# Experts sorted by token count with windows of 232 to 168 columns, and up projections as pairs of a double-width and a single-width matmul

## The chip, the cores and the metric

One core of one Trainium2 chip. The metric is device microseconds (us) of one execution, the median of several; lower is better. The core's engines run their own instruction queues in order and wait for one another through semaphores: PE (TensorE, matmuls, with its weight loads PEld), DVE (VectorE), ACT (ScalarE), POOL (GpSimd), and SP, which issues most of the transfers.

## The reference, cut to what matters

Three stages follow one another; each takes the output of the one before. The middle one is the subject.

```python
attn_out = _attn_ref(q, k, v, lam)                  # decay attention, 2 x 8 heads x 768 x 64
x = attn_out.transpose(0, 2, 1, 3).reshape(1536, 512)
# _moe_ref: N, D, E, F = 1536, 512, 8, 1024
expert_idx = np.argmax(x @ w_gate, axis=1)          # each token goes to one of 8 experts
for e in range(E):
    mask = expert_idx == e
    h = np.maximum(x[mask] @ w1[e], 0.0)            # "up", 512 -> 1024
    out[mask] = gate_w[mask, None] * (h @ w2[e])    # "down", 1024 -> 512
# _moe2_ref: h = x @ w_in (512 -> 2048), Mish, @ w_out
```

## The kernel before

Attention runs until about 87 us. As it goes, tokens are routed: each row of its output is scattered by an indirect transfer into a DRAM table `bins` with one region per expert, in order of arrival. The MoE stage runs from 86.9 to 262.9 us, the FFN from there to 531.5 us.

An fp32 product is made of three products in a faster format: each operand is split into a high part (`hi`, ACT, L189) and the rest (`lo`, DVE or POOL, L194), and hi*hi, hi*lo and lo*hi are summed in PSUM. Weights come in pieces of 128x1024 (`raw`, `load_piece`, L182), eight for an expert, alternately of w1 and w2.

Each expert works on a fixed window of 232 token columns (`WIN`). The loop over g = 4*e + c (e the expert, c a quarter of its 1024 hidden columns) records for each g, in this order:

- `up(g)`: 24 matmuls of 232 columns (L719) into one PSUM tile `h` of tag "a", of which there are three. Then ACT writes relu of it as the high part of `hh` (L722) and DVE the low part (L723).
- at c = 3 the second half of the next expert's transposes (`turn_x(e+1, 1)`).
- `down(g-1)`: eight pairs of matmuls. The first (L740) takes the high weights against `hh` high and low side by side, 464 columns, into the two halves of a PSUM tile `y`; the second (L743) takes the low weights against `hh` high, 232 columns, into the second half. At c = 3 ACT copies one half to the sums `Y` (L747) and DVE adds the other (L748), four times.
- at g = 1 `clear_y` (L619 to L623: two memsets of `Y` on DVE, one each on ACT and POOL), the `pad` scatters that write zeros behind each expert's tokens (POOL), at c = 2 the first half of the next expert's transposes: `turn_x` (PE transposes L701 into a PSUM tile of tag "c", of which there is one; ACT L266 and DVE L267 split it), `advance` (the splits of two weight pieces), `load_x` (L689, the next expert's 256 rows of `bins` into `xw`), and for 9 values of g from 8 to 24 with c = 0 or 1 a conversion of FFN weights (`narrow`: ACT L139, DVE L140, L141, L146).

`tables()` (L647 to L664), 13 small DVE instructions, stands ahead of the loop, and computes offsets and slots from the counts. The buffers of weights and other large tiles are 33 units in rotation, so a load waits for the last reader of the unit that it takes. All engines take their instructions in the order in which they are recorded. An expert with more tokens than its window is finished by a loop behind the program's end; with this input's counts (195, 205, 194, 205, 168, 157, 227, 185) it isn't entered.

Of the kernel before, what the change touches and what calls it, by code (L numbers as in the profile page):

```python
# [39 lines left out]
REST = WIN - P  # L40
FF = 2048
# [5 lines left out]
NX = -(-NT // WIN) - 1  # L47
# [13 lines left out]
def kernel(  # L61
# [52 lines left out]
    cmax = const.tile([P, NE], F32, name="cmax")  # L114
# [50 lines left out]
    with tc.manual_schedule():  # L165
# [9 lines left out]

        def load_piece():
# [93 lines left out]
        with ExitStack() as actx:  # L270
# [95 lines left out]
            def constants():  # L366
                for i, (n, b) in enumerate(STEPS):
                    POOL.iota(tok[:, i:i + 1], pattern=[[0, 1]], base=b * SEQ + n * P, channel_multiplier=1)
                POOL.iota(
                    steps, pattern=[[WIN, NX]], base=WIN, channel_multiplier=0, allow_small_or_imprecise_dtypes=True)  # L370
# [3 lines left out]
                POOL.memset(ones8, 1.0)  # L374
                POOL.memset(zeros, 0.0)
# [210 lines left out]
            for _ in range(5):  # L586
                load_piece()
# [58 lines left out]

        def tables():  # L647
            DVE.tensor_tensor_scan(out=incl, data0=ones8, data1=base, initial=0.0, op0=ALU.mult, op1=ALU.add)
            DVE.tensor_tensor(out=off_f, in0=incl, in1=base, op=ALU.subtract)
# [357 lines left out]
```

## Time and profile before

| | |
|---|---|
| time, 3 runs | 542.29 us median (541.59 to 542.36) |
| profiled execution | 541.75 us, of which the span of the trace is 540.1 us |
| PE busy | 522.6 us (97%) |
| DVE, ACT, POOL busy | 369.8 (68%), 324.7 (60%), 185.2 us (34%) |
| DMA | 74.98 MB, mean 139 GB/s |

PE's share is that of the whole span. What DVE and ACT do matters where PE waits for them; the rows below show where that is, and how long single instructions take.

### The profile page before, as it was taken

How to read it: one execution, taken by the hardware profiler on the slowest of the kernel's cores; microseconds unless marked ns; L12 is line 12 of the kernel's file. 1: busy time of each engine (PE TensorE's matmuls, PEld its weight loads, DVE VectorE, ACT ScalarE, POOL GpSimd, SP SyncE). 2: the span in 40 equal slices, each digit the busy share in tenths (PEclk: the TensorE clock that was granted, in tenths of full speed). 3: DMA queues.
4: the chain of work that ended last, by engine and by line, in shares of the span. 5: the costliest groups of instructions: out<-in, count | busy, mean ns of one | idle time of the engine just before them, and what ended most of it. 6: DMA issues, size and time to landing. Idle time of an engine off the chain costs nothing. (4 is left out here: it accounts for less than half of the span.)

```text
span 540.1 us, 8441 instructions
## 1 busy us (share of the span) xinstructions
PE 522.6 (97%) x3101; PEld 451.4 (84%) x3102; DVE 369.8 (68%) x668; ACT 324.7 (60%) x514; POOL 185.2 (34%) x151
## 2 busy tenths in 40 slices
PE   8999988999999999999999999999999999999993
PEld 5888878999999999999788878888888888888882
DVE  7999965765967858653498776567965778436362
ACT  1566533655674566555678876777666775765650
POOL 7788842755573331235100321003210031103032
PEclk9999999999999999999999999999999999999997
DMA  8999837119999996731301024020230000001022
GB/s 259 340 329 332 277 147 292 52 49 399 315 299 224 223 360 236 262 128 40 118 0 62 18 79 133 23 79 0 95 139 4 0 0 1 0 1 58 21 80 81
DMA packets 28944, 74.98 MB, mean 139 GB/s; under 512 B 6652, under 2 KB 6652, under 8 KB 28896
## 3 DMA queue, kind: packets, MB, share of 16 engines
q1 hardware_dynamic: 25040, 66.62, 38.3%
q0 software_dynamic: 3424, 7.23, 3.6%
q8 instruction: 26, 0.43, 0.4%
q10 hardware_dynamic: 432, 0.53, 0.3%
q14 instruction: 22, 0.18, 0.1%
HBM read 66.61 MB, written 10.49 MB: 143 GB/s over the span
## 5 line engine op out<-in xcount | busy, mean ns | idle before, releaser
L194 POOL TENSOR_TENSOR lo_f<-w,hi_f 128x1024 fp32r<-128x1024 f32 x16 | 39.8, 2487 | 185.9 <-ACT hi_f L189 155.1
L719 PE MATMUL h<-x,hi_w 128*128 128x232 f32 x512 | 87.5, 274 | 0.0
L740 PE MATMUL y<-hh,hi_w 128*128 128x464 f32 x256 | 84.8, 380 | 0.9 <-DVE hh L723 0.9
L796 PE MATMUL hp<-yt,hi_f 128*128 128x512 f32 x256 | 79.3, 391 | 0.0
L719 PEld LDWEIGHTS h<-x,hi_w 128*128 128x128 f32 x512 | 77.8, 192 | 0.0
L828 PE MATMUL acc<-hi_f,ghi 128*128 128x512 f32 x192 | 76.2, 397 | 0.4 <-ACT Y L833 0.4
L828 PE MATMUL acc<-hi_f,glo 128*128 128x512 f32 x192 | 75.8, 395 | 0.0
L828 PE MATMUL acc<-lo_f,ghi 128*128 128x512 f32 x192 | 75.7, 394 | 0.0
L136 DVE TENSOR_TENSOR t<-t,hp 128x512 f32<-128x512 f32 x48 | 32.8, 684 | 61.1 <-ACT t L135 61.1
L719 PE MATMUL h<-x,lo_w 128*128 128x232 f32 x256 | 71.1, 278 | 0.0
L743 PE MATMUL y<-hh,lo_w 128*128 128x232 f32 x256 | 69.1, 270 | 0.0
L194 DVE TENSOR_TENSOR lo_w<-raw,hi_w 128x1024 fp32r<-128x1024 f32 x50 | 63.0, 1283 | 7.5 <-ACT hi_w L189 6.9
L132 ACT ACTIVATE t<-hp 128x512 f32<-128x512 f32 x48 | 28.6, 600 | 62.4 <-PE hp L796 62.1
L189 ACT ACTIVATE hi_w<-raw 128x1024 fp32r<-128x1024 f32 x64 | 64.5, 1055 | 0.9 <-DMA raw<-in_w1p_dram 0.9
L194 POOL TENSOR_TENSOR lo_w<-raw,hi_w 128x1024 fp32r<-128x1024 f32 x14 | 35.1, 2510 | 71.5 <-ACT hi_w L189 70.8
L796 PEld LDWEIGHTS hp<-yt,hi_f 128*128 128x128 f32 x256 | 48.1, 188 | 11.1
L740 PEld LDWEIGHTS y<-hh,hi_w 128*128 128x128 f32 x256 | 48.2, 188 | 6.1 <-DVE hh L723 1.1
L796 PE MATMUL hp<-yt,lo_f 128*128 128x512 f32 x128 | 50.4, 394 | 0.0
L719 PEld LDWEIGHTS h<-x,lo_w 128*128 128x128 f32 x256 | 49.0, 191 | 0.5
L743 PEld LDWEIGHTS y<-hh,lo_w 128*128 128x128 f32 x256 | 48.9, 191 | 0.0
L722 ACT ACTIVATE hh<-h 128x464 fp32r<-128x464 f32 x32 | 17.8, 558 | 49.7 <-PE h L719 45.2
L723 DVE SCALAR_TENSOR_TENSOR hh<-h,hh 128x464 fp32r<-128x464 f32 x32 | 20.4, 639 | 34.8 <-ACT hh L722 34.8
(163 smaller groups left out, 1032.9 us busy)
## 6 DMA issues: line engine op xcount, KB each, us to landing
raw<-in_w1p_dram SPq DMA_DIRECT2D x32, 512.0 KB
raw<-in_w2p_dram SPq DMA_DIRECT2D x32, 512.0 KB
w<-in_w3p_dram SPq DMA_DIRECT2D x32, 512.0 KB
xw<-bins SPq DMA_DIRECT2D x7, 512.0 KB
qbd<-in_qT_dram SPq DMA_DIRECT2D x24, 128.0 KB
v_n<-in_vN_dram SPq DMA_DIRECT2D x12, 256.0 KB
k_n<-in_kN_dram SPq DMA_DIRECT2D x10, 256.0 KB
k_t<-in_kT_dram SPq DMA_DIRECT2D x10, 256.0 KB
```

Source lines behind the costliest of these rows:

```text
L132: yield lambda: ACT.activation(out=t, in_=h, func=AF.Tanh, scale=0.5)
L136: yield lambda: DVE.tensor_tensor(out=t, in0=t, in1=h, op=ALU.mult)
L189: ACT.activation(out=hi, in_=r, func=AF.Copy)
L194: engine.tensor_tensor(out=lo, in0=r, in1=hi.bitcast(F32), op=ALU.subtract)
L719: PE.matmul(out=p[:, m, :], lhsT=w[:, s], rhs=x[k // 2][:, k % 2, r, :], start=(k == 0 and m == 0 and z == 0), stop=(k == KD - 1 and z == ...
L722: ACT.activation(out=h[:, :, 0, :], in_=p, func=AF.Relu)
L723: DVE.scalar_tensor_tensor(out=h[:, :, 1, :], in0=p, scalar=0.0, in1=h[:, :, 0, :].bitcast(F32), op0=ALU.max, op1=ALU.subtract)
L740: PE.matmul(out=y.rearrange("p z n -> p (z n)"), lhsT=whi[:, s], rhs=h[:, f].rearrange("p z n -> p (z n)"), start=(c == 0 and f == 0), sto ...
L743: PE.matmul(out=y[:, 1, :], lhsT=wlo[:, s], rhs=h[:, f, 0, :], start=False, stop=(c == 3 and f == 1), skip_group_check=True)
L796: PE.matmul(out=p, lhsT=w[:, s], rhs=x, start=(k == 0 and z == 0), stop=(k == KD - 1 and z == 2))
L828: PE.matmul(out=acc[t], lhsT=x[:, s], rhs=w[:, DM:2 * DM], start=(first and z == 0), stop=(last and z == 2))
```

## The change

The windows become `WINS = (232, 232, 232, 212, 200, 192, 180, 168)`. Experts 0 and 1 stay; the other six are taken by falling count, so that place 2 is the expert with most tokens. Which expert stands at a place is known on the chip alone, so `tables()` computes it (23 DVE instructions; those for left-over tokens are moved to g = 26), and SP loads `who_i` into registers and addresses weights and `bins` with them.

`up` now makes eight pairs like those of `down`: the first 128 hidden columns (m = 0) into one PSUM tile of tag "a", the second (m = 1) into another. Of each tile ACT copies one half to SBUF (L794) and DVE adds the other (L795); then come ACT's relu (L796) and DVE's low part (L797), now from that SBUF tile. `down` follows two groups behind instead of one. The transposes of expert 1 are both recorded at g = 2; those of later experts one group earlier than before (c = 1 and 2). Two weight pieces instead of five are preloaded at the end of attention.

```diff
-                for k0 in range(0, KD, 2):
-                    for m in range(2):
-                        for k in (k0, k0 + 1):
-                            s = slice(k * FC + m * P, k * FC + (m + 1) * P)
-                            for z, (w, r) in enumerate(((wlo, 0), (whi, 0), (whi, 1))):
-                                PE.matmul(out=p[:, m, :], lhsT=w[:, s], rhs=x[k // 2][:, k % 2, r, :],
...
-                ACT.activation(out=h[:, :, 0, :], in_=p, func=AF.Relu)
+                w = WINS[e]
+                h = hs[g] = ep.tile([P, 2, 2, WIN], F32R, tag="h", name=f"hh{g}", bufs=3)[:, :, :, 0:w]
+                p = [ps.tile([P, 2, WIN], F32, tag="a", name=f"h{g}_{m}", bufs=3)[:, :, 0:w] for m in range(2)]
+                t = ep.tile([P, 2, WIN], F32, tag="t", name=f"hs{g}", bufs=2)[:, :, 0:w]
+                for m in range(2):
+                    for k in range(KD):
+                        s = slice(k * FC + m * P, k * FC + (m + 1) * P)
+                        xk = x[k // 2][:, k % 2]
+                        PE.matmul(out=p[m], lhsT=whi[:, s], rhs=xk, start=(k == 0), stop=False,
+                                  skip_group_check=True)
+                        PE.matmul(out=p[m][:, 1, :], lhsT=wlo[:, s], rhs=xk[:, 0, :],
+                                  start=False, stop=(k == KD - 1), skip_group_check=True)
+                    ACT.activation(out=t[:, m, :], in_=p[m][:, 1, :], func=AF.Copy)
+                    DVE.tensor_tensor(out=t[:, m, :], in0=p[m][:, 0, :], in1=t[:, m, :], op=ALU.add)
+                ACT.activation(out=h[:, :, 0, :], in_=t, func=AF.Relu)
...
-            for g in range(NG + 1):
+            for g in range(NG + 2):
                 if g < NG:
                     up(g)
-                    if g % 4 == 3:
-                        turn_x(g // 4 + 1, 1)
-                if g > 0:
-                    down(g - 1)
+                if g > 1:
+                    down(g - 2)
...
+                    if g == 2:
+                        turn_x(1, 0)
+                        turn_x(1, 1)
+                    elif g > 4 and g % 4 in (1, 2):
+                        turn_x(g // 4 + 1, g % 4 - 1)
                     advance(2 * g + 7)
-                    if g % 4 == 0 and g > 0:
-                        load_x(g // 4 + 1)
+                    if g == 4:
+                        load_x(2)
+                    elif g > 4 and g % 4 == 3:
+                        load_x(g // 4 + 2)
```

On PE, around the transposes of expert 1 (`t_0`, `t_1`; `xw` are its rows), before: between the two stand the 24 matmuls of up(3), of which the first is shown.

```order
L701 MATMUL t_0_1432<-ident,xw_1248 128x128
L701 MATMUL t_0_1432<-ident,xw_1248 128x104
L701 MATMUL t_0_1432<-ident,xw_1248 128x128
L701 MATMUL t_0_1432<-ident,xw_1248 128x104
L719 MATMUL h_1448<-x_0_1221,lo_w_868 128x232
...
L701 MATMUL t_1_1476<-ident,xw_1248 128x128
```

The same place after, behind down(0):

```order
L771 MATMUL t_0_1434<-ident,xw_1262 128x128
L771 MATMUL t_0_1434<-ident,xw_1262 128x104
L771 MATMUL t_0_1434<-ident,xw_1262 128x128
L771 MATMUL t_0_1434<-ident,xw_1262 128x104
L771 MATMUL t_1_1442<-ident,xw_1262 128x128
L771 MATMUL t_1_1442<-ident,xw_1262 128x104
L771 MATMUL t_1_1442<-ident,xw_1262 128x128
L771 MATMUL t_1_1442<-ident,xw_1262 128x104
L790 MATMUL h_0_1458<-x_0_1235,hi_w_887 128x464
```

The second transposes follow the first at once now, and both use the one PSUM tile of tag "c".

On DVE, the first rows behind `tables()`, before (`h_...` the PSUM tiles of up(0), up(1) and up(2), `x_0` the split of `t_0`):

```order
L723 SCALAR_TENSOR_TENSOR hh_1269<-h_1270,hh_1269 128x2x232
L723 SCALAR_TENSOR_TENSOR hh_1309<-h_1310,hh_1309 128x2x232
L621 MEMSET Y_1237 128x1768
L622 MEMSET Y_1238 128x1768
L194 TENSOR_TENSOR lo_w_1374<-raw_865,hi_w_1373 128x1024
L194 TENSOR_TENSOR lo_w_1378<-raw_952,hi_w_1377 128x1024
L723 SCALAR_TENSOR_TENSOR hh_1381<-h_1382,hh_1381 128x2x232
L267 TENSOR_TENSOR x_0_1431<-t_0_1432,x_0_1431 128x2x232
```

The same place after (`hs` is the SBUF tile of the sums):

```order
L795 TENSOR_TENSOR hs_1334<-h_0_1332,hs_1334 128x232
L795 TENSOR_TENSOR hs_1334<-h_1_1333,hs_1334 128x232
L797 SCALAR_TENSOR_TENSOR hh_1331<-hs_1334,hh_1331 128x2x232
L650 MEMSET Y_1251 128x1768
L651 MEMSET Y_1252 128x1768
L221 TENSOR_TENSOR lo_w_1374<-raw_885,hi_w_1373 128x1024
L221 TENSOR_TENSOR lo_w_1378<-raw_972,hi_w_1377 128x1024
L795 TENSOR_TENSOR hs_1384<-h_0_1382,hs_1384 128x232
L795 TENSOR_TENSOR hs_1384<-h_1_1383,hs_1384 128x232
L797 SCALAR_TENSOR_TENSOR hh_1381<-hs_1384,hh_1381 128x2x232
L294 TENSOR_TENSOR x_0_1433<-t_0_1434,x_0_1433 128x2x232
L294 TENSOR_TENSOR x_1_1441<-t_1_1442,x_1_1441 128x2x232
```

The order is the old one with two adds ahead of each low part; `x_1` now stands directly behind `x_0`.

On DVE after, in a group of expert 3 with c = 1 (up(13), then the sums of expert 2, four adds of L822 of which one is shown, then the transposes of expert 4):

```order
L795 TENSOR_TENSOR hs_2155<-h_0_2153,hs_2155 128x212
L795 TENSOR_TENSOR hs_2155<-h_1_2154,hs_2155 128x212
L797 SCALAR_TENSOR_TENSOR hh_2152<-hs_2155,hh_2152 128x2x212
...
L822 TENSOR_TENSOR Y_1251<-y_0_1980,Y_1251 128x232
...
L294 TENSOR_TENSOR x_0_2220<-t_0_2221,x_0_2220 128x2x200
L221 TENSOR_TENSOR lo_w_2231<-raw_2129,hi_w_2230 128x1024
L221 TENSOR_TENSOR lo_w_2237<-raw_2135,hi_w_2236 128x1024
L155 TENSOR_SCALAR sb_2147<-w_1_1_1854 128x512
L156 SCALAR_TENSOR_TENSOR sb_2147<-w_1_1_1854,sb_2147 128x512
L161 SCALAR_TENSOR_TENSOR w_1_2146<-w_1_2146,sb_2147 128x512
```

Before, the split `x_0` stood a group later, with fewer instructions beside it, and there were no adds of L795.

## Rows read from the trace of the kernel before

**Rows 1.** PE, PEld, DVE, ACT, POOL busy in 20 us of MoE; PEclk, DMA share, GB/s:

```profile
140.00:160.00 20.00, 20.00 (x159) 19.41 (x158) 14.98 (x20) 11.29 (x19) 14.75 (x9) 1.00 0.97 310
```

**Rows 2.** Timeline of PE, within up: start, us, instructions:

```profile
113.21 0.27 PE L719 MATMUL h<-x,lo_w 128*128 128x232 f32 x1
...
113.55 0.27 PE L719 MATMUL h<-x,lo_w 128*128 128x232 f32 x1
```

**Rows 3.** Timeline of PE, within down:

```profile
110.31 0.38 PE L740 MATMUL y<-hh,hi_w 128*128 128x464 f32 x1
110.52 0.27 PE L743 MATMUL y<-hh,lo_w 128*128 128x232 f32 x1
110.62 0.38 PE L740 MATMUL y<-hh,hi_w 128*128 128x464 f32 x1
```

**Rows 4.** Timeline of PE's weight loads, same place:

```profile
110.31 0.19 PEld L743 LDWEIGHTS y<-hh,lo_w 128*128 128x128 f32 x1
...
110.63 0.19 PEld L743 LDWEIGHTS y<-hh,lo_w 128*128 128x128 f32 x1
```

**Rows 5.** Timeline of PE, first matmuls and the same line later:

```profile
2.47 3.60 PE L288 MATMUL idle<-warm 128*128 128x512 bf16 x8 [2.47 <-DVE warm L285]
5.86 4.83 PE L393 MATMUL a<-qbd,k_t 128*128 128x256 f32 x16
24.41 1.97 PE L393 MATMUL a<-qbd,k_t 128*128 128x256 f32 x8
```

**Rows 6.** Timeline of PE, first matmul of the MoE and first of down:

```profile
86.93 0.43 PE L719 MATMUL h<-x,lo_w 128*128 128x232 f32 x1
...
93.57 0.48 PE L740 MATMUL y<-hh,hi_w 128*128 128x464 f32 x1 [0.91 <-DVE hh L723]
```

**Rows 7.** Timeline of DVE, start of the MoE; in brackets idle time before, and releaser:

```profile
88.47 0.17 DVE L648 TENSOR_TENSOR_SCAN incl<-ones,base 128x8 f32<-128x8 f32 x1
...
90.66 0.17 DVE L664 TENSOR_TENSOR pos_i<-pos_f,slot_f 128x12 int32<-128x12 f32 x1
92.87 1.19 DVE L723 SCALAR_TENSOR_TENSOR hh<-h,hh 128x464 fp32r<-128x464 f32 x2 [2.04 <-ACT hh L722]
94.38 1.53 DVE L621 MEMSET Y<- 128x1768 f32 x1 [0.32 <-issue]
...
97.68 2.29 DVE L194 TENSOR_TENSOR lo_w<-raw,hi_w 128x1024 fp32r<-128x1024 f32 x2
```

**Rows 8.** Timeline of ACT, first relu of the MoE:

```profile
92.28 1.00 ACT L722 ACTIVATE hh<-h 128x464 fp32r<-128x464 f32 x2 [4.41 <-DMA raw<-in_w1p_dram]
```

**Rows 9.** Timeline of SP: the rows of experts 1 and 2, merged:

```profile
92.56 27.29 SPq L689 DMA_DIRECT2D xw<-bins  x2
```

**Rows 10.** Engines' busy time behind the last matmul, columns as in rows 1:

```profile
533.50:534.00 0.50, 0.00 (x0) 0.00 (x0) 0.00 (x0) 0.00 (x0) 0.00 (x0) 0.92 0.11 41
534.00:534.50 0.50, 0.00 (x0) 0.00 (x0) 0.00 (x0) 0.00 (x0) 0.00 (x0) 0.50 0.96 360
```

**Rows 11.** Last matmul, from the timeline of PE:

```profile
531.11 0.40 PE L828 MATMUL acc<-lo_f,ghi 128*128 128x512 f32 x1
```

**Rows 12.** Groups by line of DVE and ACT, 100 to 260 us: busy, mean ns:

```profile
L194 DVE TENSOR_TENSOR lo_w<-raw,hi_w 128x1024 fp32r<-128x1024 f32 x40 | 51.0, 1302 | 7.5 <-ACT hi_w L189 6.9 <-issue 0.6
...
L189 ACT ACTIVATE hi_w<-raw 128x1024 fp32r<-128x1024 f32 x54 | 54.1, 1055 | 0.0
L722 ACT ACTIVATE hh<-h 128x464 fp32r<-128x464 f32 x29 | 16.2, 558 | 42.9 <-PE h L719 42.8
```

**Rows 13.** Timeline of DVE, a group with sums and a conversion:

```profile
177.56 0.71 DVE L748 TENSOR_TENSOR Y<-y,Y 128x232 f32 x2 [0.17 <-issue]
...
180.12 2.36 DVE L194 TENSOR_TENSOR lo_w<-raw,hi_w 128x1024 fp32r<-128x1024 f32 x2 [0.60 <-issue]
182.40 0.42 DVE L140 TENSOR_SCALAR sb<-w 128x512 int32<-128x512 int32 x1
...
184.07 0.63 DVE L723 SCALAR_TENSOR_TENSOR hh<-h,hh 128x464 fp32r<-128x464 f32 x1
```

More of the change, by code (lines that the diff above doesn't have):

```diff
@@ L113 @@
     first_i = const.tile([P, NE, NX], I32, name="first_i")
-    cmax = const.tile([P, NE], F32, name="cmax")
+    key = const.tile([P, NE], F32, name="key")
+    above = const.tile([P, NSORT, NSORT], F32, name="above")
+    rank = const.tile([P, NSORT], F32, name="rank")
+    sel = const.tile([P, NSORT, NSORT], F32, name="sel")
+    part = const.tile([P, NSORT, NSORT], F32, name="part")
+    count = const.tile([P, NE], F32, name="count")
+    who_f = const.tile([P, NSORT], F32, name="who_f")
+    who_i = const.tile([P, NSORT], I32, name="who_i")
+    at_f = const.tile([P, NE], F32, name="at_f")
+    wins = const.tile([P, NE], F32, name="wins")
+    thr = const.tile([P, NE], F32, name="thr")
+    over_f = const.tile([P, NE, NX], F32, name="over_f")
+    cmax = const.tile([P, 8], F32, name="cmax")
     cmax_i = const.tile([P, 1], I32, name="cmax_i")
@@ L174, with expert @@
         n_load, n_split = [0], [0]
+        experts = {}
+        def expert(e):
+            if e not in experts:
+                j = e - (NE - NSORT)
+                experts[e] = SP.value_load(who_i[0:1, j:j + 1], min_val=0, max_val=NE - 1)
+            return experts[e]
         def load_piece():
@@ L374, in constants @@
                 POOL.memset(ones8, 1.0)
+                for j, w in enumerate(WINS):
+                    POOL.memset(wins[:, j:j + 1], float(w - OWIN))
                 POOL.memset(zeros, 0.0)
@@ L585 @@
             SP.dma_start(out=first, in_=bins[0, 0:ROWS].rearrange("(a p) d -> p a d", p=P))
-            for _ in range(5):
+            for _ in range(2):
                 load_piece()
@@ L625, with split_y @@
         yt = {}
-        def split_y(yp, th, ks):
+        def split_y(where, th, ks):
             for k in ks:
-                hi = yp.tile([P, TH], F32R, tag=f"yhi{k}", name=f"yhi{th}_{k}", bufs=1)
-                lo = yp.tile([P, TH], F32R, tag=f"ylo{k}", name=f"ylo{th}_{k}", bufs=1)
+                if where is None:
+                    t = unit([P, 2, TH], F32R, f"yt{th}_{k}")
+                else:
+                    t = where.tile([P, 2, TH], F32R, tag=f"yt{k}", name=f"yt{th}_{k}", bufs=1)
                 src = Y[k // 2][:, k % 2, th * TH:(th + 1) * TH]
-                ACT.activation(out=hi, in_=src, func=AF.Copy)
-                DVE.tensor_tensor(out=lo, in0=src, in1=hi.bitcast(F32), op=ALU.subtract)
-                yt[th, k] = (hi, lo)
+                ACT.activation(out=t[:, 0, :], in_=src, func=AF.Copy)
+                DVE.tensor_tensor(out=t[:, 1, :], in0=src, in1=t[:, 0, :].bitcast(F32), op=ALU.subtract)
+                yt[th, k] = (t[:, 0, :], t[:, 1, :])
         def split_later(th, k):
@@ L912, in overflow @@
             DVE.tensor_copy(out=xt[:, 2 * g:2 * g + 2, :], in_=p)
-        h = op.tile([P, NE, WIN], F32, name="o_h")
-        y = [ps.tile([P, 2, WIN], F32, tag=f"y{i}", name=f"o_y{i}", bufs=1) for i in range(2)]
+        h = op.tile([P, NE, OWIN], F32, name="o_h")
+        y = [ps.tile([P, 2, OWIN], F32, tag=f"y{i}", name=f"o_y{i}", bufs=1) for i in range(2)]
         for c in range(4):
@@ L920, in overflow @@
             for m in range(2):
-                p = ps.tile([P, WIN], F32, tag="h", name=f"o_h{c}_{m}", bufs=2)
+                p = ps.tile([P, OWIN], F32, tag="h", name=f"o_h{c}_{m}", bufs=2)
                 for k in range(KD):
```

125 lines of the change are left out of this document (80 added, 45 removed).

## The prediction

> **What bounds the kernel now.** First the busy time by stretches [rows 1]: in the middle of the MoE PE is busy for 20.00 of 20 us at a granted clock of 1.00, that is 2.4 GHz. DVE stands at 14.98. So PE sets the pace, and a matmul saved there is time saved, as long as the other engines keep up with a shorter stage. DVE has only a quarter of the time left, and its work is uneven. The timelines of PE then give the unit prices. In up, three matmuls of 232 columns take 113.55 - 113.21 = 0.34 us, 112 ns each [rows 2]. In down, a pair of 464 and 232 columns takes 110.62 - 110.31 = 0.32 us (0.3225 over several), 215 and 107 ns [rows 3]. The time before in the profiled execution is 541.75 us; it lies 0.5 us below the median of the runs shown, so I sum against 541.75 and add 0.5 for the median. About 0.2%, 1.1 us, is what a measurement of this kernel can tell from no change.
>
> **What PE saves.** (a) A group's up has 24 matmuls of 112 ns, 2.69 us; as eight pairs of 0.3225 it is 2.58. Over 32 groups that is 3.5 us. (b) Narrowing. The windows of places 3 to 7 miss 20, 32, 40, 52 and 64 columns, 208 together, and an expert has 64 pairs. The double-width matmul loses 416 columns in sum, so 416 x 64 / 2.4 GHz = 11.1 us. What the single-width one gains is bounded from both sides: nothing, or another 208 x 64 / 2.4 = 5.5 us. I take nothing. The weight load of the matmul behind it starts together with it, and weight loads lie 0.32 us apart for two [rows 4]; in up, where one load and one 232-column matmul alternate, the pitch is 112 ns though 232 columns at 2.4 GHz are 97 ns. A load of 128 columns thus seems to need about 107 ns by itself, whatever the matmul beside it.
>
> The Trainium skill bears on this (TensorE: Matmul & The Clock Gate, "LDWEIGHTS (loading the stationary operand)"): a weight load takes its columns divided by 1.2, some 107 ns for 128, independent of what moves. The pitch here agrees; by that rule the narrowing gives 11.1 us, and without it 16.6.
>
> The two-part moving operand itself I cost at nothing: line 393 has a moving operand of two parts of 128 columns, and eight of these take 1.97 us [rows 5], 0.22 us after overlap for an fp32 matmul of 256 columns, no more than their columns ask; a penalty would be seen there. (c) The shorter transposes save 208 x 4 columns, 0.3 us. (d) PE's wait of 0.91 us for the first `hh` [rows 6] falls into the waits costed below. Together **-15.8 us**.
>
> **What the start costs.** Three PSUM tiles of tag "a" now hold one and a half groups. PE begins at 86.93 [rows 6]; three halves of 1.29 us end at 90.8. The fourth needs the first tile back, and that is released by the add of L795, which on DVE stands behind `tables()`. These go from 88.47 to 90.83 with 13 instructions [rows 7], 0.18 us each; with 23, some on 36 elements, they end near 92.8. The copies on ACT ahead of the add come no sooner: ACT's first relu starts at 92.28, held by a transfer [rows 8]. With an add of 0.4 us PE goes on at 93.2: **+2.3**.
>
> Next the two transposes of expert 1. PE then does three halves and down(0), and `t_0`, until 100.1. `t_1` needs the one tile of tag "c" back, hence DVE's split `x_0`. On DVE ahead of that stand the adds and low parts of g = 0 and 1 (until about 96.6), the two memsets (94.38 to 97.68, 3.3 us with their gaps) and two low parts of weights (2.29) [rows 7], then the adds, the wait for relu and the low part of g = 2: 96.6 + 3.7 + 2.3 + 1.9 + 0.6 = 105.2. PE waits from 100.1 to 105.2: **+5.1**. Before, up(3) stood between the two transposes and covered this. Bounds: 3 where DVE catches up between, 7 with longer gaps. If this wait were gone, the next would take much of it: the rows of expert 2 are loaded as the second of two transfers that end their issue at 92.56 + 27.29 = 119.85 [rows 9], behind the pads; it would stand a few us earlier now, and PE would reach its transposes at 114 without the waits, at 121 with them.
>
> An idle PE can lose its clock. At the end the last matmul starts at 531.11 [rows 11], and the granted clock falls from 1.00 to 0.50 (1.2 GHz) at 533.9 [rows 10], under 3 us later; the wait above is 5 us. What a slow start costs is seen at the kernel's beginning: eight matmuls of 512 columns take 3.60 us and the next sixteen 4.83 us [rows 5], where at the rate of their later row and of rows 3 they would take 1.9 and 3.9: 2.6 us lost. Between 0 and 2.6 I take **+1.3**.
>
> **What DVE and ACT cost in experts 3 to 6.** Now each group's DVE work is a round trip: two adds (0.71 for two of 232 columns [rows 13]), the wait for ACT's relu on their sum (0.56), then the low part (0.63) while ACT makes the high weights (1.06) [rows 12], then low weights, and where due a conversion. In order on DVE, at 212 columns:
> - c = 0: 0.7 + 0.5 + 1.05 + 2.3 for two low weights + 1.67 (182.40 to 184.07 [rows 13]) = 6.2
> - c = 1: 0.7 + 0.5 + 0.6 + 2.4 for the sums (2.56 from 177.56 to 180.12 [rows 13], narrower) + 0.6 for `x_0` + 2.3 + 1.67, less 0.2 overlap = 8.6
> - c = 2: 0.7 + 0.5 + 1.05 + 1.2 for one low weight, + 0.6 for `x_1` = 4.05
> - c = 3: the same without `x_1` = 3.5
>
> That is 22.3 us for the expert of 212 columns, 22.0 and 21.8 for the next two, 20.3 for the one of 180 columns, which has one conversion less: 86.4. PE's own time is 64 pairs of (2w / 2.4 + 22 + 107) ns and 0.8 us of transposes: 20.4, 19.7, 19.3 and 18.6, in sum 78.0. DVE is 8.4 us short. PE may run ahead by a down and half an up (2.58 + 1.29 us) less a copy and an add, some 3.4 us, before it needs a tile back: **+5.0** remain. Bounds: 0 (the waits inside the round trip shrink, since ACT runs ahead) and 11 (ACT, which gets two copies a group as well, is late too).
>
> ACT's extra copies, POOL's eight memsets, the register loads on SP and the left-over tables at g = 26 lie beside PE's work; the two pieces instead of five come before they are read, since loads are two groups (9 us) ahead. FFN and attention are unchanged.
>
> **Sum.** -15.8 + 2.3 + 5.1 + 1.3 + 5.0 = -2.1: 539.65 profiled, **540.2 us** as median.
>
> **The rivals.** *DVE keeps up.* Speaking for it: its busy time, with 2.9 us of adds per expert, is some 18.8 of 20 us; against it, the order, in which every add has a wait behind it. Without the 5.0: 535.1. *The weight load is no floor:* up to 5.5 less on PE, but of these 3.8 fall into experts 3 to 6 where DVE is short; about 538.5, or 529.7 if DVE keeps up as well. (The rule of the Trainium skill's page TensorE: Matmul & The Clock Gate, cited above, excludes it.) *On the other side, DVE and ACT are slower by turns.* ACT's copy of m = 1 stands behind high weights and conversions, DVE's add waits for it, and ACT's relu waits for the add. It decides from 0.2 us more per group: 16 groups by 0.2 are 3.2 us, which takes the time over 543.4. At 0.5 us per group it is +8: 548; with 0.3, 545. *The order on the chip doesn't help:* a count over its window would start the loop behind the end, tens of us; the counts in falling order, 227, 205, 194, 185, 168, 157, leave 5 to 12 columns, so this is nearly excluded.
>
> **How the numbers follow.** My forecast 0.37 (538 to 543), DVE keeps up 0.27 (533 to 538), no floor 0.05, slower round trip 0.29, overflow 0.02. Faster by over 0.2% (under 541.2): two thirds of the first case, all of the second and third, 0.58. Within 0.2%: 0.09 of the first and 0.04 of the fourth, 0.13. Slower: 0.29. A range from 533 to 547 leaves out the low end of the second and third and the far end of the fourth, about 0.2.
>
> **What would show it.** Pairs in up at 0.32 us and at 168 columns near 0.27 (0.25 without a floor). PE idle of 2 us behind the third half, released by DVE's add, and of 5 us between `t_0` and `t_1`, released by DVE's `x_0`, with matmuls of double length behind it if the clock falls. In experts 3 to 6 PE idle of 1 to 2 us per expert, released by DVE L795 or L797, mostly in c = 1 and 2, and DVE without idle there. The prediction is wrong if PE stays at 20.00 of 20 us there, or if ACT ends these waits.

## The result and the profile after

The changed kernel takes **549.17 us** (median of 4 runs, 548.06 to 550.33), the kernel before in the same comparison 541.94 (541.33 to 542.36): ratio 1.0135 [1.011, 1.0159]. It is slower, by 7.2 us, and lies beyond the range of the forecast. The profiled execution took 548.06 us, the shortest of the four, and is 6.3 us longer than that of the kernel before. In its page PE has lost its full share (94% busy, 97% before):

```profile
PE 516.1 (94%) x2845; PEld 442.0 (81%) x2846; DVE 399.5 (73%) x749; ACT 338.1 (62%) x578; POOL 186.1 (34%) x159
```

The MoE stage, taken from its first up matmul to the first matmul of the FFN, went from 175.60 us (86.93 to 262.53) to 182.67 (86.61 to 269.28): +7.07, so the loss is in it; the other two stages together were 0.8 us shorter in this execution. In 20-us windows, with the columns of [rows 1], PE is idle for 0.6 to 1.9 us in each of the five from 147 us on, and DVE is busy for 17 to 18, where [rows 1] had 14.98; the three short windows at half clock come with them:

```profile
94.00:97.00 3.00, 3.00 (x12) 2.71 (x11) 1.35 (x3) 1.33 (x4) 2.07 (x2) 0.50 0.01 0
106.50:110.50 4.00, 4.00 (x15) 3.71 (x15) 2.23 (x3) 2.81 (x4) 3.34 (x3) 0.50 0.16 55
248.00:250.50 2.50, 2.50 (x12) 2.50 (x11) 2.08 (x4) 2.27 (x4) 0.49 (x1) 0.50 0.00 0
...
127.00:147.00 20.00, 20.00 (x129) 18.65 (x128) 15.27 (x20) 12.56 (x23) 10.65 (x6) 1.00 0.92 283
147.00:167.00 20.00, 18.72 (x120) 17.43 (x119) 17.64 (x25) 14.09 (x26) 11.95 (x7) 1.00 0.87 220
...
227.00:247.00 20.00, 18.14 (x124) 17.00 (x122) 17.77 (x32) 10.97 (x24) 5.28 (x2) 1.00 0.69 227
```

The timeline of PE shows where the idle time stands, in brackets with its releaser, and the prices that answer to [rows 2] and [rows 3]:

```profile
91.45 0.27 PE L792 MATMUL h<-x,lo_w 128*128 128x232 f32 x1
93.45 0.47 PE L790 MATMUL h<-x,hi_w 128*128 128x464 f32 x1 [1.74 <-DVE hs L795]
...
94.34 0.61 PE L790 MATMUL h<-x,hi_w 128*128 128x464 f32 x1
...
106.30 1.03 PE L771 MATMUL t<-ident,xw 128*128 128x128 f32 x4 [4.15 <-DVE x L294]
...
154.58 0.48 PE L790 MATMUL h<-x,hi_w 128*128 128x464 f32 x1 [1.28 <-DVE hs L795]
...
168.61 0.52 PE L771 MATMUL t<-ident,xw 128*128 128x128 f32 x4
168.93 0.44 PE L790 MATMUL h<-x,hi_w 128*128 128x424 f32 x1
...
176.79 0.46 PE L790 MATMUL h<-x,hi_w 128*128 128x424 f32 x1 [1.11 <-DVE hs L795]
...
190.13 0.94 PE L771 MATMUL t<-ident,xw 128*128 128x128 f32 x4
190.99 0.45 PE L790 MATMUL h<-x,hi_w 128*128 128x400 f32 x1
...
220.49 0.44 PE L790 MATMUL h<-x,hi_w 128*128 128x384 f32 x1 [0.96 <-DVE hs L795]
...
247.24 0.42 PE L790 MATMUL h<-x,hi_w 128*128 128x336 f32 x1 [1.88 <-DVE hs L795]
...
252.16 0.35 PE L790 MATMUL h<-x,hi_w 128*128 128x336 f32 x1
...
252.43 0.35 PE L790 MATMUL h<-x,hi_w 128*128 128x336 f32 x1
```

The waits are 6.6 us before 115 us (0.73, 1.74 and 4.15), and 6.1 behind 150 us: 1.28, 1.11, 0.64 and 0.96 in the last group (c = 3) of experts 2 to 5, 0.22 in expert 6, and 1.88 in the first group of expert 7. All of the late ones but the 0.22 are released by DVE's add L795. Two more things are to be seen. Four transposes take 168.93 - 168.61 = 0.32 us where their second part has 72 rows (the expert of 200 columns), and 190.99 - 190.13 = 0.86 us where it has 64 (192 columns). And the clock falls three times.

DVE's timeline at the start answers to [rows 7]; the second part is around the wait at 154.58. Below it POOL's timeline of the same stretch:

```profile
92.34 0.17 DVE L714 TENSOR_TENSOR pos_i<-pos_f,slot_f 128x12 int32<-128x12 f32 x1
...
105.61 0.63 DVE L294 TENSOR_TENSOR x<-t,x 128x464 fp32r<-128x464 f32 x1
...
150.28 2.62 DVE L155 TENSOR_SCALAR sb<-w 128x512 int32<-128x512 int32 x1
...
155.49 0.64 DVE L797 SCALAR_TENSOR_TENSOR hh<-hs,hh 128x464 fp32r<-128x464 f32 x1 [0.66 <-ACT hh L796]
...
159.41 1.43 DVE L797 SCALAR_TENSOR_TENSOR hh<-hs,hh 128x464 fp32r<-128x464 f32 x1 [0.66 <-ACT hh L796]
...
163.18 1.53 DVE L797 SCALAR_TENSOR_TENSOR hh<-hs,hh 128x424 fp32r<-128x424 f32 x1 [0.63 <-ACT hh L796]
...
169.84 0.60 DVE L797 SCALAR_TENSOR_TENSOR hh<-hs,hh 128x424 fp32r<-128x424 f32 x1 [0.62 <-ACT hh L796]
```

```profile
150.13 2.48 POOL L221 TENSOR_TENSOR lo_w<-raw,hi_w 128x1024 fp32r<-128x1024 f32 x1 [4.72 <-ACT hi_w L216]
...
157.86 2.48 POOL L221 TENSOR_TENSOR lo_w<-raw,hi_w 128x1024 fp32r<-128x1024 f32 x1 [4.11 <-ACT hi_w L216]
...
161.74 2.52 POOL L221 TENSOR_TENSOR lo_w<-raw,hi_w 128x1024 fp32r<-128x1024 f32 x1
```

The same low part takes 0.60 to 0.64 us alone (155.49, 169.84) and 1.43 to 1.53 while POOL splits weights (159.41 to 160.8 inside POOL's 157.86 to 160.34; 163.18 inside 161.74 to 164.26). The conversion at 150.28, 2.62 us instead of 0.41, also lies beside POOL. In the kernel before, conversions and DVE's own weight splits were stretched like this already, but not the low part:

```profile
137.44 2.64 DVE L140 TENSOR_SCALAR sb<-w 128x512 int32<-128x512 int32 x1
...
141.28 3.19 DVE L194 TENSOR_TENSOR lo_w<-raw,hi_w 128x1024 fp32r<-128x1024 f32 x1
...
149.17 0.64 DVE L723 SCALAR_TENSOR_TENSOR hh<-h,hh 128x464 fp32r<-128x464 f32 x1 [0.53 <-ACT hh L722]
```

This L723 at 149.17 stood beside a weight split of POOL as well (148.42 to 150.92), and kept 0.64 us. It reads `h` from PSUM; L797 reads `hs` and `hh`, both in SBUF. The L194 at 141.28 reads `raw` and `hi_w`, both in SBUF: it took 3.19 us beside POOL's split of 140.97 to 143.39, where two of them at 180.12, with POOL not splitting, took 2.36 together [rows 13]. So the trace of the kernel before held the row that shows what an instruction of DVE with both inputs in SBUF costs beside POOL.

### The profile page after: what moved, and what is told of

Same layout as the page of the kernel before. It is cut to its first block, busy times and chain, and to the rows that moved or that the text cites. A ratio compares the mean times of both kernels' runs of the same rounds, so it can differ in the third digit from the quotient of the medians.

```text
span 546.3 us, 8197 instructions
## 1 busy us (share of the span) xinstructions
PE 516.1 (94%) x2845; PEld 442.0 (81%) x2846; DVE 399.5 (73%) x749; ACT 338.1 (62%) x578; POOL 186.1 (34%) x159
## 4 chain that ended last, share of the span: by engine, by line
PE 58%; DVE 14%; ACT 6%; issue 4%; DMA 2%; SPq 0%; DVEq 0%; ACTq 0%; POOLq 0%; POOL 0%
PE acc L907 24%; PE hp L875 24%; DVE lo_w L221 5%; PE h L790 4%; PE y L815 3%; DVE hs L795 2%; ACT hi_w L216 2%; DMA xw<-bins 2%; PE h L792 2%; PE y L817 1%; ACT hh L796 1%; DVE sb L155 1%; DVE w L161 1%; DVE sb L156 1%; DVE x L294 1%
## 5 line engine op out<-in xcount | busy, mean ns | idle before, releaser
L875 PE MATMUL hp<-yt,hi_f 128*128 128x512 f32 x384 | 119.7, 392 | 0.0
L790 PE MATMUL h<-x,hi_w 128*128 128x464 f32 (+5 forms) x256 | 84.9, 387 | 8.3 <-DVE hs L795 7.6
L875 PEld LDWEIGHTS hp<-yt,hi_f 128*128 128x128 f32 x384 | 72.1, 188 | 17.2 <-DVE yt L664 0.9
L815 PE MATMUL y<-hh,hi_w 128*128 128x464 f32 (+5 forms) x256 | 79.8, 371 | 0.2 <-DVE Y L822 0.2
L875 PE MATMUL hp<-yt,lo_f 128*128 128x512 f32 x192 | 75.7, 394 | 0.3 <-ACT yt L663 0.3
L792 PE MATMUL h<-x,lo_w 128*128 128x232 f32 (+5 forms) x256 | 67.8, 265 | 0.0
L817 PE MATMUL y<-hh,lo_w 128*128 128x232 f32 (+5 forms) x256 | 66.4, 259 | 0.0
L790 PEld LDWEIGHTS h<-x,hi_w 128*128 128x128 f32 x256 | 50.2, 196 | 13.2 <-DVE hs L795 9.1
L796 ACT ACTIVATE hh<-hs 128x464 fp32r<-128x464 f32 (+5 forms) x32 | 17.6, 549 | 49.1 <-DVE hs L795 49.1
L797 DVE SCALAR_TENSOR_TENSOR hh<-hs,hh 128x464 fp32r<-128x464 f32 (+5 forms) x32 | 29.7, 927 | 19.7 <-ACT hh L796 19.7
```

The lines of the kernel that those rows point to most:

```text
L790: PE.matmul(out=p[m], lhsT=whi[:, s], rhs=xk, start=(k == 0), stop=False, skip_group_check=True)
L792: PE.matmul(out=p[m][:, 1, :], lhsT=wlo[:, s], rhs=xk[:, 0, :], start=False, stop=(k == KD - 1), skip_group_check=True)
L796: ACT.activation(out=h[:, :, 0, :], in_=t, func=AF.Relu)
L797: DVE.scalar_tensor_tensor(out=h[:, :, 1, :], in0=t, scalar=0.0, in1=h[:, :, 0, :].bitcast(F32), op0=ALU.max, op1=ALU.subtract)
L815: PE.matmul(out=y, lhsT=whi[:, s], rhs=h[:, f], start=(c == 0 and f == 0), stop=False, skip_group_check=True)
L817: PE.matmul(out=y[:, 1, :], lhsT=wlo[:, s], rhs=h[:, f, 0, :], start=False, stop=(c == 3 and f == 1), skip_group_check=True)
```

## The experiments

Each kernel starts from the changed one unless it says otherwise. "Stage" is the MoE stage as above, waits are PE's idle time in it.

**The transposes with 104 rows again** (x1_rows): the second part takes all of the loaded rows, and the copies out of PSUM use the w columns.

```diff
-                    for a, n in enumerate((P, w - P)):
+                    for a, n in enumerate((P, REST)):
...
-                split_x(p, x)
+                split_x(p[:, :, 0:w], x)
```

> The changed kernel with one edit: the second transposes of every expert always take 104 rows (as before) instead of 84, 72, 64, 52 and 40; the split still reads only the window's columns. In the changed kernel four transposes take 0.32 us up to a second part of 72 rows and 0.82 to 0.87 us from 64 rows down. Theory (64 rows or fewer cost PE a pause at each change): all groups of four at 0.33 to 0.35 us, six of them 0.5 us shorter, time 3 us less than the changed kernel, 546. Rival (the long transposes stand where DVE sets the pace anyway, so their time is only moved into waits): under 1 us less.

549.27 us, 1.0133 [1.0104, 1.0162]: the same as the changed kernel's 549.17. The timeline of PE in x1_rows, at the 192-column expert:

```profile
196.31 0.56 PE L771 MATMUL t<-ident,xw 128*128 128x128 f32 x4
196.66 0.43 PE L790 MATMUL h<-x,hi_w 128*128 128x400 f32 x1
...
199.50 0.45 PE L790 MATMUL h<-x,hi_w 128*128 128x400 f32 x1 [1.44 <-DVE hs L795]
```

Four transposes take 0.35 us again, so 64 rows or fewer are what made them 0.86. But the wait behind them is 1.44 where it was 0.64, and all waits behind 150 us grew from 6.1 to 8.5. The slow transposes mostly filled time in which PE would have waited for DVE: the rival was right.

**The second transposes of expert 1 behind up(3)** (x2_late), where they stood before.

```diff
                     up(g)
+                    if g == 3:
+                        turn_x(1, 1)
...
                         turn_x(1, 0)
-                        turn_x(1, 1)
```

> The changed kernel with one edit: the second transposes of expert 1 are recorded behind up(3), as before, not directly behind the first. Theory: the wait of 4.15 us between the two is covered by up(3), and the fall of the clock behind it doesn't come; together 6 us less than the changed kernel, 543. Rival: the wait only moves, since DVE is as late for the low parts of g = 2 and the rows of expert 2 come no earlier: under 2.5 us less, with a new wait of 3 to 4 us at down(1) or at the transposes of expert 2.

545.94 us, 1.0067 [1.004, 1.0094]: 3.2 us better than the changed kernel, where the theory had 6. PE's timeline in x2_late:

```profile
105.00 0.48 PE L790 MATMUL h<-x,hi_w 128*128 128x464 f32 x1 [1.57 <-DVE hs L795]
...
107.16 0.62 PE L771 MATMUL t<-ident,xw 128*128 128x128 f32 x4 [0.62 <-DVE x L294]
...
112.25 0.48 PE L790 MATMUL h<-x,hi_w 128*128 128x464 f32 x1 [1.22 <-DVE x L294]
```

The wait of 4.15 became three of 3.4 together: DVE is late there whatever PE asks it for. The waits give only 0.8 us of the gain. The clock stayed at 1.00 from 90 to 130 us in this execution; in the changed kernel it stood at 0.50 for two stretches there.

**POOL without its weight splits** (x3_nopool): for the 14 pieces that POOL splits in the MoE, the high part stands in for the low one.

```diff
-                pieces[i] = halves(r, f"w{i}", POOL if i in ON_POOL else DVE)
+                if i in ON_POOL:
...
+                    pieces[i] = (hi, hi)
```

> The changed kernel without POOL's 14 low parts of MoE weights: those pieces use their high part in place of the low one, so part of the weights' precision is left out; DVE's own work is the same. In the changed kernel DVE's low part L797 takes 0.51 to 0.64 us alone and 1.4 to 1.6 us whenever such an instruction of POOL runs. Theory (two operands in SBUF make it wait for POOL): all L797 at 0.51 to 0.65, waits of PE in experts 2 to 7 fall from 6.1 us to under 1.5, no fall of the clock at 247 us, time 6 to 8 us less, 541 to 543. Rival (as forecast: the round trip of add, relu and low part is too long in itself): L797 shorter, but PE's waits at c = 1 and 2 stay above 4 us and the time is 2 us less.

545.77 us, 1.0045 [1.0024, 1.0066]. That is 3.4 us better than the changed kernel, where the theory had 6 to 8. All low parts of `hh` took 0.51 to 0.66 us until 250 us, and behind 154 us PE waited no more. The waits at the start stayed (6.4 us), and behind them is one stall of 2.7 us (2.05 and 0.64), with a fall of the clock. It stands behind this row of DVE in x3_nopool, a conversion whose weights came late; below it is PE's:

```profile
150.00 0.43 DVE L155 TENSOR_SCALAR sb<-w 128x512 int32<-128x512 int32 x1 [4.92 <-DMA w<-in_w3p_dram]
```

```profile
151.51 0.47 PE L795 MATMUL h<-x,hi_w 128*128 128x464 f32 x1 [2.05 <-DVE hs L800]
```

Leaving out POOL's splits also left out their buffers, so the transfers came in another order; that this made it late was not settled. z3_free below keeps the buffers.

**A warm PE** (x4_warm): 36 matmuls with a zero moving operand between the two transposes of expert 1, which keep PE busy during the wait of 4.15 us.

```diff
+                        for _ in range(36):
+                            PE.matmul(out=ys[0][0][:, 0, :], lhsT=still[:, 0:P], rhs=still, start=False, stop=False,
+                                      skip_group_check=True)
```

> The changed kernel with 36 extra matmuls of zeros (232 columns, about 0.1 us each) between the two transposes of expert 1, added to a sum that they don't change: they fill the wait of 4.15 us and take nothing from it. Theory (an idle PE loses its clock, and pays about 2.4 us behind this wait): the matmuls behind it start at 0.32 us a pair instead of 0.60, granted clock 1.00 in 106 to 112 us, time 2 to 2.5 us less than the changed kernel. Rival (the slow pairs come from something else, such as the weights' arrival): pairs stay at 0.60 and the time is the same.

The window behind the wait, in x4_warm:

```profile
112.00:114.00 2.00, 1.40 (x10) 1.33 (x11) 0.69 (x2) 0.73 (x2) 1.67 (x2) 1.00 0.08 33
```

The clock stayed at 1.00, pairs took 0.32 us, and the stage was 3.5 us shorter (179.18). In this execution the clock fell nowhere in the stage, so that not all of the 3.5 us is due to the edit. The time was nonetheless 551.41, 1.0165 [1.0142, 1.0188], since attention ended 7.1 us later (the stage began at 93.70 instead of 86.61). Two falls of the clock in attention, of 3.4 us each at 0.50, are part of that; the rest is open.

**The sums in PSUM** (x5_psum): DVE adds into the PSUM tile, and relu and low part read from there, for each m.

```diff
-                    DVE.tensor_tensor(out=t[:, m, :], in0=p[m][:, 0, :], in1=t[:, m, :], op=ALU.add)
+                    DVE.tensor_tensor(out=p[m][:, 0, :], in0=p[m][:, 0, :], in1=t[:, m, :], op=ALU.add)
```

> The changed kernel with one edit: DVE's add of L795 writes its sum back to PSUM, and relu and low part are made for each half of 128 hidden columns from there, so that the low part has one operand in SBUF and one in PSUM. POOL keeps its 14 low parts. Theory (low parts with both operands in SBUF wait for POOL's instruction): no low part of hh over 0.45 us, PE's waits in experts 2 to 7 fall from 6.1 us to under 1.5, no fall of the clock at 247 us; MoE stage 7 us shorter than the changed kernel's 182.7. Rival (the round trip itself is too long, and PSUM tiles now come free later): waits stay at 4 us or more, stage at most 3 us shorter.

544.92 us, 1.0042 [1.0027, 1.0057], between the two. The low parts were free of POOL, but a PSUM tile of tag "a" now comes free only behind its low part: PE waited 4.4 us in experts 2 to 7, released by `hh` instead of `hs`. The theory had under 1.5 us left and a stage 7 us shorter; it was 2.9 us shorter (179.82), as the rival said.

**The three repairs and later memsets** (x7_clear): x1, x2 and x5 together, and `clear_y` at g = 4 instead of 1.

```diff
-                    if g == 1:
+                    if g == 4:
                         clear_y()
```

> The changed kernel with four edits together: second transposes with 104 rows, transposes of expert 1 apart again, sums in PSUM as in the run beside it, and the clearing of Y moved from g = 1 to g = 4. If waits, clock and slow transposes are what the narrow windows lost, all three go: MoE stage near 165 us against 175.6 before and 182.7 changed, time 531 to 534, faster than both kernels. Rival (DVE stays the bound of experts 3 to 6, since it has as many instructions): stage at 172 to 175, time 539 to 542.

543.98 us, 1.0036 [1.0023, 1.005]: the start costs 3.2 us of waits instead of 6.6, but experts 2 to 7 still 6.4, and the clock fell three times in the stage for 3.4 us each. The stage is 176.21 us, and neither theory nor rival had it. With these repairs the pairs of up remain behind the kernel before.

**Narrow windows alone** (y1_narrow): the kernel before with its single matmuls in up and its fixed order of experts, windows written down for this input's counts, 104-row transposes.

```diff
+WINS = (232, 232, 200, 212, 180, 168, 232, 192)
...
-                p = ps.tile([P, 2, WIN], F32, tag="a", name=f"h{g}", bufs=3)
+                p = ps.tile([P, 2, WIN], F32, tag="a", name=f"h{g}", bufs=3)[:, :, 0:n]
```

> The kernel before with fixed windows of 232 to 168 columns, the same eight widths as in the change, each put on the expert whose count fits it; no sorting, up as 24 single matmuls, no adds, second transposes with 104 rows. Theory (weight loads of 128 columns are a floor of about 107 ns, so single matmuls of 112 ns gain almost nothing, and only the double-width ones of down do): up 2.69 to about 2.6 us a group, down 2.58 to 2.12 at 168 columns, MoE stage 6 to 7 us shorter than 175.6, time 535.5. Rival (no floor): up 2.0 us at 168 columns, stage 13 us shorter.

**536.46 us, 0.9885 [0.987, 0.9901]**, and PE never waits in the stage, which takes 168.43 us instead of 175.60. PE's timeline in y1_narrow, in an up of the expert of 168 columns:

```profile
200.08 0.38 PE L721 MATMUL h<-x,hi_w 128*128 128x168 f32 x2
...
200.41 0.39 PE L721 MATMUL h<-x,hi_w 128*128 128x168 f32 x2
...
200.75 0.39 PE L721 MATMUL h<-x,hi_w 128*128 128x168 f32 x2
```

Three single matmuls of 168 columns take 0.335 us, those of 232 took 0.34 [rows 2]. So a single matmul gains next to nothing from fewer columns. Of the 7.2 us by which the stage is shorter, the double-width matmuls of down give 416 x 32 / 2.4 GHz = 5.5, and 0.9 is the wait that the kernel before had. The time is only 5.6 us below that of the kernel before in the same comparison (542.04); in the traced execution the clock stood at 0.50 for 6.8 us in attention, ahead of the stage.

**Wide windows with everything else** (y2_wide): all of WINS 232 in the changed kernel.

> The changed kernel with all windows at 232 columns: sorting, register loads, pairs and adds stay. PE's matmuls take 11 to 12 us more. Theory (what narrowing saves on PE is given back in waits of experts 3 to 7, with the clock that falls there, and in transposes of 64 rows or fewer): these 6 + 1.6 + 3 us go, so the MoE stage is the changed kernel's within 2 us, 182 to 185, time 549 to 551. Rival (the narrow windows pay in full and the loss is all from pairs and start): stage 11 us longer, time 560.

554.57 us, 1.0236 [1.0214, 1.0257], so the narrowing is worth 5.4 us in the changed kernel, half of the 11.1 us that it takes off PE's matmuls; both forecasts missed. The late waits are again at most one an expert, 4.3 us behind 150 us. A PE that keeps the old widths meets a late DVE too: the narrowing alone is not what makes DVE late.

**Single matmuls in up** (z4_singles: this alone; z1_sorted: also x1, x2 and the late `clear_y`). The experts stay sorted.

```diff
-                p = [ps.tile([P, 2, WIN], F32, tag="a", name=f"h{g}_{m}", bufs=3)[:, :, 0:w] for m in range(2)]
...
+                p = ps.tile([P, 2, WIN], F32, tag="a", name=f"h{g}", bufs=3)[:, :, 0:w]
...
+                ACT.activation(out=h[:, :, 0, :], in_=p, func=AF.Relu)
```

> The changed kernel with up alone put back to 24 single matmuls and no adds; all else as in the change, the transposes of expert 1 side by side and those with 64 rows or fewer too. Theory (the adds and what they wait for lose more than the pairs win): on PE 9 us more for the matmuls, but no waits from expert 2 on, so that the stage is 175 to 178 and the time 542 to 545, 4 to 7 us less than the changed kernel; the wait between the transposes of expert 1 stays at 3.5 to 5 us. Rival (the pairs are worth their 9 us and the start is the loss): stage 188 or more.

> The changed kernel with up put back to 24 single matmuls into one PSUM tile and no adds; sorting, register loads, narrow windows and the lag of two groups stay; second transposes with 104 rows, transposes of expert 1 apart, clearing of Y at g = 4. Theory (sorting costs nothing beside PE, single matmuls leave DVE enough room that POOL's instructions don't matter): MoE stage that of the fixed narrow windows, 168 to 170, time 536 to 538, faster than the kernel before by about 1%. Rival (sorting by register, or the later tables, cost a wait of their own): stage 172 or more.

z4_singles: 545.69 us (10 runs from 542.39 to 550.43), 1.0058 [1.0032, 1.0085]; z1_sorted: 542.51 (12 runs), 1.0 [0.9989, 1.0011]. The stages are 182.82 us in z4_singles, whose traced execution is one of its longest (550.15), and 176.13 in z1_sorted: both theories had less. But in both PE has no wait behind 130 us, with POOL's splits in place: it is the pairs of up, with their adds, that make DVE late in experts 2 to 7. Both kernels also show what was hidden behind the start's waits, a wait for the rows of expert 2 (3.47 us in z4_singles), in PE's timeline of z1_sorted and a window behind it:

```profile
119.59 1.01 PE L771 MATMUL t<-ident,xw 128*128 128x128 f32 x4 [4.65 <-DMA xw<-bins]
```

```profile
122.00:124.00 2.00, 2.00 (x11) 2.00 (x11) 1.83 (x2) 1.08 (x2) 0.00 (x0) 0.50 1.05 422
```

The rows of expert 2 are there at 119.6 us; the forecast said that they would be the next wait if the one at 106 were gone. The clock falls as well.

**The same with later transposes** (z5_turn): z1_sorted with every `turn_x` a group later, as before the change.

```diff
+                    if g % 4 == 3:
+                        turn_x(g // 4 + 1, 1)
...
+                    if g % 4 == 2:
+                        turn_x(g // 4 + 1, 0)
```

> The sorted kernel with single matmuls (stage 176.1 us, with one wait of 4.65 us for the rows of expert 2 at the transposes of g = 5 and slow matmuls behind it), with one edit: all transposes stand where they stood before the change, a group later. Theory (the rows of expert 2 land near 119.5 us, and the change asks for them at 115): no wait over 0.5 us, granted clock 1.00 throughout, stage 168 to 170, time 535 to 537, faster than the kernel before by 1.0 to 1.3%. Rival (register-addressed loads are late throughout): the wait moves to g = 6, stage 173 or more.

**535.6 us, 0.9869 [0.9853, 0.9885]**: faster than both kernels, with the experts sorted on the chip. PE is not idle once in the stage (168.47 us), and the clock stays at 1.00. A window of z5_turn:

```profile
207.00:227.00 20.00, 20.00 (x164) 20.00 (x164) 14.53 (x26) 11.60 (x19) 5.15 (x2) 1.00 0.83 280
```

**Pairs in up, repaired at the start, without and with POOL's splits** (z3_free, z6_pool): both have x1, x2 and the late `clear_y`. z3_free lets the high part stand in for POOL's low parts and keeps their buffers; z6_pool differs from it in this alone.

```diff
-                if i in ON_POOL:
-                    hi, lo = high(r, f"w{i}")
-                    POOL.memset(lo[:, 0:1].bitcast(F32), 0.0)
-                    pieces[i] = (hi, hi)
...
+                pieces[i] = halves(r, f"w{i}", POOL if i in ON_POOL else DVE)
```

> The changed kernel, pairs and adds included, with second transposes of 104 rows, transposes of expert 1 apart, clearing of Y at g = 4, and without POOL's 14 low parts of MoE weights (the high part stands in for them, so precision is left out; their buffers are still taken). Theory (start, slow transposes and POOL's instructions beside DVE are the whole loss): matmuls 154 + transposes 5 + 2 to 4 at the start, stage 161 to 164, time 528 to 531. Rival (DVE's own chain is too long for pairs in experts 2 to 6): waits of 4 us or more there, stage 168 or more.

> The changed kernel with pairs and adds, second transposes of 104 rows, transposes of expert 1 apart and clearing of Y at g = 4: the run without POOL's low parts (MoE stage 169.8 us, three waits of 1.41, 0.83 and 1.18 us in experts 3 to 5, time 535.4), with POOL's low parts put back. If POOL's instructions beside DVE cost what the run without them in the first round showed, 4 to 6 us: stage 174 to 176, time 540 to 542, waits of 7 us or more in experts 2 to 7. If DVE's own order makes nearly all the waits: stage within 2 us of 169.8, time 535 to 537.

z3_free 535.36 us, 0.9863 [0.9846, 0.9881]; z6_pool 543.08, 1.0016 [0.9999, 1.0032]. The stage went from 169.80 to 177.28 us and its waits behind 130 us from 3.7 to 10.1. PE's longest late wait, z6_pool, then z3_free:

```profile
242.58 0.42 PE L790 MATMUL h<-x,hi_w 128*128 128x336 f32 x1 [2.18 <-DVE hs L795]
```

```profile
171.96 0.46 PE L795 MATMUL h<-x,hi_w 128*128 128x424 f32 x1 [1.41 <-DVE hs L800]
```

DVE's groups by shape from 155 to 235 us, z6_pool, then z3_free (busy, mean ns, idle before):

```profile
L797 DVE SCALAR_TENSOR_TENSOR hh<-hs,hh 128x424 fp32r<-128x424 f32 x4 | 4.2, 1052 | 2.5 <-ACT hh L796 2.5
L797 DVE SCALAR_TENSOR_TENSOR hh<-hs,hh 128x400 fp32r<-128x400 f32 x4 | 4.2, 1052 | 2.4 <-ACT hh L796 2.4
...
L155 DVE TENSOR_SCALAR sb<-w 128x512 int32<-128x512 int32 x7 | 2.9, 417 | 0.0
```

```profile
L155 DVE TENSOR_SCALAR sb<-w 128x512 int32<-128x512 int32 x7 | 2.9, 420 | 0.0
L802 DVE SCALAR_TENSOR_TENSOR hh<-hs,hh 128x424 fp32r<-128x424 f32 x4 | 2.4, 601 | 2.5 <-ACT hh L801 2.5
L802 DVE SCALAR_TENSOR_TENSOR hh<-hs,hh 128x400 fp32r<-128x400 f32 x4 | 2.3, 576 | 2.4 <-ACT hh L801 2.4
```

The low part takes 1052 ns in the mean with POOL's splits and 576 to 601 without (over the stage 13 of the 32 take 1.25 to 1.60 us in z6_pool, 2 in z3_free); the waits for ACT's relu (2.4 to 2.5) and the conversions of this stretch are the same. In sum the 32 low parts take 30.9 us with POOL's splits and 20.7 without. The 7.7 us between these two kernels (7.5 in the stage) are what POOL's splits cost here; PE's late waits are 6.4 of them, mostly released by DVE's add.

## Why the prediction was wrong

It said 540.2 with 0.29 for slower. Three of its terms failed: the price of DVE's low part (0.63 us, measured up to 1.6 beside POOL), the clock (one fall of up to 2.6 us, measured three and 5.8), and the transposes (a saving of 0.3 us, measured a cost of 3.1). By its own steps, in the profiled execution:

| step | forecast | measured |
|---|---|---|
| matmuls: up as pairs, narrowing | -14.6 | -15.2 |
| transposes | -0.3 | +3.1 |
| before's own wait | -0.9 | -0.9 |
| waits at the start | +7.4 | +6.6 |
| clock | +1.3 | +5.8 |
| late waits: forecast in experts 3 to 6, measured in 2 to 7 | +5.0 | +6.1 |
| not itemised | 0 | +1.6 |
| sum (measured: of the stage) | -2.1 | +7.1 |

*Matmuls: right.* Pairs measure 0.3225 us at 232 columns and 0.265 at 168 (eight from 252.16 to 254.28 in 2.12 us). With 0.306, 0.294, 0.2875 and 0.277 for the widths between, 64 x (3 x 0.3225 + 0.306 + 0.294 + 0.2875 + 0.277 + 0.265) = 153.4 us against 32 x (2.69 + 2.58) = 168.6. The weight load is a floor: in y1_narrow the single matmul stays and the pair shrinks. The operand of two parts costs nothing: at 212 columns, where it has two, a pair takes 0.306 us, 0.0165 less than at 232, where the two lie side by side as one, and 40 columns at 2.4 GHz are 0.0167. The row that this was argued from [rows 5] does not show it, since 0.22 us for 256 columns is twice what 2.4 GHz gives.

*Start: right in place and size.* `tables()` ended at 92.51 (forecast 92.8), `x_0` at 106.24 (105.2), and the rows of expert 2 were the next wait, in z1_sorted and z4_singles.

*Transposes: a failed step.* "The shorter transposes save 208 x 4 columns, 0.3 us" priced them by columns. Six groups of four with a second part of 64, 52 or 40 rows took 0.82 to 0.87 us instead of 0.32 to 0.35. x1_rows showed that undoing this alone gives nothing, because DVE's lateness fills the place: the 3.1 us of the table and the late waits can't be added up as if each stood alone.

The Trainium skill has the rule (TensorEngine Tiling (Array Packing), "Key Properties"): a change of tiling mode drains the engine, and its "Available Configurations" have tiles of 64 rows. The trace agrees: 72 rows next to 128 cost nothing, 64 rows beside 128 cost 0.5 us for four. That the pause is such a drain is not shown, only that it comes with 64 rows or fewer and disappears with 104 (x1_rows).

*Clock: mis-sized.* The forecast allowed one fall behind one wait of 5 us, 0 to 2.6 us. There were three, at 0.50, that is 1.2 GHz: 94.0 to 97.4, 106.3 to 111, 247.6 to 251, some 11.6 us of matmuls at half rate, 5.8 us. Two of them came behind PE idles of only 1.74 and 1.88 us; at 94.00 PE had been at work again since 93.45, where in [rows 10, 11] it stayed idle until the fall. This share is that of one execution: the same idle at the start (1.73 to 1.76 us) had a fall behind it in x3_nopool, z3_free and z6_pool too, and none in x1_rows, x2_late, x4_warm and y2_wide.

*Late waits: the size nearly, by luck; the cause half.* The releaser (L795) is as foretold. The place is not: the forecast put 5.0 us into experts 3 to 6, mostly at c = 1 and 2, and there 2.9 were measured, at c = 3 but for 0.2; the other 3.2 stand in experts 2 and 7. And the cycle was worked out with "the low part (0.63)", the duration that the row of the kernel before shows, for an instruction whose operand had moved from PSUM to SBUF. In z6_pool it takes 1.05 us in the mean at 200 and 212 columns; without POOL's splits the waits are 3.7 us, less than the 5.0 forecast for the order on DVE alone, and with them 10.1. In the changed kernel they are 6.1; x1_rows (8.5) shows that the slow transposes hide 2.4, and what hides the rest was not tried.

The Trainium skill states this too (SBUF — State Buffer, "Who interferes with whom"): an instruction of DVE with two inputs in SBUF contends with one of GpSimd that reads SBUF, and one with at most one such input, outside the modes that take both ports, does not. The trace agrees: L797 0.6 against 1.43 to 1.53, and L723 with one operand in PSUM 0.64 beside POOL.

*The rivals.* "DVE and ACT are slower by turns" had the right sign and the wrong mechanism: ACT's copies held DVE's adds for only 2.3 us in all from 100 to 260 us, and not where PE waited. "DVE keeps up" (535.1) is near z3_free (535.36), but not by its path: z3_free has POOL's splits left out, the start repaired, and late waits of 3.7 us. "No floor" is refuted by y1_narrow.

*What decides.* z5_turn and z6_pool have the same windows, sorting and 104-row transposes, but single matmuls against pairs in up (and transposes a group apart): 535.6 against 543.08. At these windows the pairs save PE some 9 us (32 groups of 2.68 us against 32 x 8 pairs of 0.265 to 0.3225), not only the 3.5 of equal windows, and lose more by DVE: the stage is 177.28 against 168.47. The narrowing gives the 5.5 us of down in full where nothing waits (y1_narrow), and 5.4 of its 11.1 in the changed kernel. The sorting costs nothing once the transposes stand late: y1_narrow, whose order is fixed, has the same stage (168.43) as z5_turn (168.47).

*Open:* the 1.6 us not itemised, though a group of up with a wait in it takes about 0.3 us more than the wait (174.22 to 178.10 us: 3.87 less 1.11 is 2.76, against 2.43 for such a group without one); when a short idle lowers the clock and when it doesn't; most of why attention took longer in x4_warm; the late transfer in x3_nopool; and whether pairs with the later transposes of z5_turn would keep up, which was not run. That a slow start, the clock and DVE add up in the changed kernel is a reading of one trace; what POOL's splits, the short transposes, the early second transposes of expert 1 and the pairs cost was measured each time between two kernels that differ in nothing else.

## What to carry to other kernels

Before an instruction's duration is taken over from a row, look where its operands will lie afterwards: the same low part cost 0.6 us with one operand in PSUM and up to 1.6 with both in SBUF beside a busy POOL, and with thirteen of those a gain of 7 us (z3_free) was none (z6_pool). Look in the trace of before for another instruction that already has its operands there; here it was the weight split of 3.19 us. Where PE is the bound and DVE has a quarter of its time left, a change that saves PE 9 us by giving DVE and ACT two more instructions each a group is priced by the round trip that it adds, not by busy time. And when several waits stand in a row, removing one shows the next (x1_rows, x2_late, z1_sorted), so repairs are measured together as well as alone.

## What was unexpected of the hardware

- Four transposes with parts of 128 and 64 rows or fewer by turns take 0.82 to 0.87 us; with 128 and 72 or 104 rows 0.32 to 0.35.
- A scalar_tensor_tensor of 128x464 with both operands in SBUF goes from 0.64 to 1.43 us beside a tensor_tensor of POOL, which itself keeps 2.5 us; a tensor_tensor of DVE of 128x1024 from 1.23 to 3.19; a tensor_scalar of 128x512 int32 goes from 0.41 to 2.62, about the length of POOL's instruction.
- The granted clock fell to 0.50 behind a PE idle of 1.74 to 1.76 us at the start of the stage in four traced executions, and not behind one of 1.73 to 1.76 in four others.
